# Attention, token mixer and gated feed-forward on one core: the first loads and the first chunks of attention in another order

## The chip, the cores and the metric

One core of a Trainium2 chip runs the whole program. The metric is the device time of one execution in microseconds (us); three runs of the kernel before took 794.02 to 795.17 us, with a median of 794.14 us.

## The reference

Inputs are q, k and v of shape (4, 8, 576, 64): 4 batches, 8 heads, 576 rows. Everything is float32 outside; the kernel works with pairs of float16 (a high and a low part) and with float32.

```python
scores = scale * q @ k^T                                # per batch and head, 576 x 576
scores = where(scores >= max(scores) - tau, scores, -1e9)
attn = exp(scores - max) ; attn /= sum(attn) + 1e-9
x = (attn @ v) with the heads side by side              # (4, 576, 512)
u = x + (relu(x^T @ w_tok1) @ w_tok2)^T                 # mixes the rows
x = u + relu(u @ w_ch1) @ w_ch2
h = relu(x @ w_in)
gate = sigmoid(conv3(h))                                # conv over rows, weights conv_w
out = (h * gate) @ w_out
```

## The kernel before

Attention runs over pairs of heads, four pairs for a batch, numbered 0 to 3 (a fifth pair is pair 0 of the next batch). A pair has nine chunks of 128 query rows, so a batch has 36 chunks, numbered 0 to 35 in batch 0. The generator `attention(b)` gives the steps of a chunk in a software pipeline, one chunk apart: `scores` (TensorE, L308), `exps` (the maximum on VectorE L324, the threshold and the exponential on ScalarE L334 and L336), `mask` (VectorE, L343), `ph` (the float16 high part on ScalarE, L348), `rest` (the low part on GpSimd, L352, then a DMA transpose issued from SyncE, L357), and five chunks later `pv` (TensorE, L367 and L370). The transposed chunk is what `pv` multiplies with v. After a pair's nine chunks, `norm` and `tok` (the token mixer, L407 and L422) follow. `dense(b)` is the rest of a batch on TensorE (L547, L565, L598, L621). For batch 0 attention runs alone; then `dense(b)` and `attention(b + 1)` are interleaved.

`prep(b, p)` brings a pair in: q (L236) and k (L240) by DMA, a scaling of q on ScalarE (L244), v by DMA (L268), then for each of the two heads a scaling of v on GpSimd (L272), its high part on ScalarE (L273) and its low part on GpSimd (L274). It stops (`yield`) between these, and `attention` runs the next piece in a later iteration.

`wload` brings a piece of the weights in: a DMA of 512 columns of 8 bytes (L118, three buffers `st`), a conversion on ScalarE and VectorE (L155 to L159), then a scaling on GpSimd (L143 or L153), the high part on ScalarE (L144) and the low part on GpSimd (L145). `W0` lists the steps of `attention(0)` at which a piece is begun.

A scheduler takes this program and sets the order on each engine; it pulls work ahead when its inputs and buffers are free. `tc.issue_after(x)` keeps what is written under it behind the instruction x. `hold` uses it to keep loads behind a transpose (`turn[i]` is the transpose of chunk i). On the chip each engine, and SyncE's queue of DMAs, works through its own order; an instruction that waits holds up all that stand behind it on its engine.

All DMAs of the first 100 us are issued by SyncE, shown as SPq.

Of the kernel before, what the change touches and what calls it, by code (L numbers as in the profile page):

```python
# [8 lines left out]
F32 = mybir.dt.float32  # L9
# [10 lines left out]
def kernel(ctx: ExitStack, tc: tile.TileContext, q, k, v, tau,  # L20
# [7 lines left out]
    nc = tc.nc  # L28
# [37 lines left out]
    V, A, G, T = nc.vector, nc.scalar, nc.gpsimd, nc.tensor  # L66


    one = const.tile([P, 1], F32, name="one")
    V.memset(one, 0.0)  # L70
    A.activation(out=one, in_=one, func=AF.Exp)
    idf = const.tile([P, P], F32, name="idf")
    make_identity(nc, idf)
    ident = const.tile([P, P], F16, name="ident")
    V.tensor_scalar_mul(ident, idf, 1.0 / UDS)
    ident2 = const.tile([P, 64], F16, name="ident2")
    V.tensor_tensor(out=ident2, in0=ident[:, 0:64], in1=ident[:, 64:P], op=ALU.add)
    blk = const.tile([P, 2, 1], F32, name="blk")
    V.memset(blk, 0.0)
    V.memset(blk[0:64, 0:1], 1.0)  # L80
    V.memset(blk[64:P, 1:2], 1.0)
    tau_t = const.tile([P, 1], F32, name="tau_t")
    nc.sync.dma_start(tau_t, tau.to_broadcast([P, 1]))

# [16 lines left out]
    wi = wpair([P, NG, NC, P], "wi")  # L103
    wo = wpair([P, NG, C], "wo")

    turn, behind, crit = {}, {}, {}

    def hold(x):
        return tc.issue_after(turn[behind[x]].ins) if behind.get(x) in turn else nullcontext()

    ps = psum.tile([P, 8, 512], F32, name="ps")
    CB = 4

    def load_hl(src, o, n):

        st = stage.tile([P, 512, 2], I32, tag="st", name="st")
        with hold("w"):
            nc.sync.dma_start(st[:, :n].rearrange("p n w -> p (n w)"), src.bitcast(I32)[:, 2 * o:2 * (o + n)])  # L118
        halves = st[:, :n].rearrange("p n w -> p (n w)").bitcast(U16).rearrange("p (n w) -> p n w", w=4)
        return halves[:, :, 1], st[:, :n, 1]  # L120
# [54 lines left out]
    def wnext():  # L175
        x = wq.pop(0)
        wrun.append(wload(*x, bank=6 if total - len(wq) <= W1 else CB))
        next(wrun[-1])

    def wstep(n):  # L180

        for _ in range(n):
            while wq and len(wrun) < 3:
                wnext()
            if wrun:
                next(wrun.pop(0))
            if wq:
                wnext()
        if n and not wrun and CB not in free:
            free.append(CB)  # L190

    cw = const.tile([P, 3 * NG], F32, name="cw")
    if conv_w.dtype == F32:
        nc.sync.dma_start(cw, conv_w)
    else:
        float32(cw, cw, *load_hl(conv_w, 0, 3 * NG), 0)
    cw = cw.rearrange("p (k g) -> p k g", k=3)


# [29 lines left out]
    def prep(b, p):  # L229

        vh, vl = v_t[p % 2]
        qt, kt = qk_t[p % 2]
        pair[b, p] = dict(qt=qt, kt=kt, vh=vh, vl=vl)
        if b < NB32:
            with hold("qk") if b else nullcontext():
                nc.sync.dma_start(f32(qt), q[b, p])  # L236
                for h in range(2):
                    if b == 0 and p < 2:
                        G.memset(f32(kt[h])[(1 - h) * D:(2 - h) * D], 0.0)
                    nc.sync.dma_start(f32(kt[h])[h * D:(h + 1) * D], k[b, p, h * D:(h + 1) * D])  # L240
            if b:
                yield
                yield
            A.activation(out=f32(qt), in_=f32(qt), func=AF.Copy, scale=qsc[:, 0:1])  # L244
        else:
            qn, kn = [qk2.tile([P, S], F32, tag="x", name="ld", bufs=15) for _ in range(2)]
            with hold("qk"):
                nc.sync.dma_start(qn, q[b, p])
                nc.sync.dma_start(kn, k[b, p])
        if b >= NB32:  # L250
            yield
            qs = qk2.tile([P, 2, S], F16, tag="x", name="qs", bufs=15)
            split(qs, qn, qsc[:, 1:2])
            for h in range(2):
                for x in range(2):
                    nc.sync.dma_start(qt[x * D:(x + 1) * D, h], qs[h * D:(h + 1) * D, x])
            yield
            ks = qk2.tile([P, 2, S], F16, tag="x", name="ks", bufs=15)
            split(ks, kn, QK)
            for h in range(2):  # L260
                for r in range(2):
                    nc.sync.dma_start(kt[h][r * D:(r + 1) * D], ks[h * D:(h + 1) * D])
        yield
        vn = []
        for hh in range(2):
            t = qk2.tile([P, S], F32, tag="x", name="ld", bufs=15)
            with hold("qk") if b else nullcontext():
                nc.sync.dma_start(t, v[b, 2 * p + hh])  # L268
            vn.append(t.rearrange("p (a d) -> p a d", d=D))
        yield  # L270
        for hh in range(2):
            G.tensor_scalar(out=vn[hh], in0=vn[hh], scalar1=VSC, scalar2=1.0, op0=ALU.mult, op1=ALU.mult)  # L272
            A.activation(out=vh[:, hh, :, 0:D], in_=vn[hh], func=AF.Copy)  # L273
            G.tensor_tensor(out=vl[:, hh], in0=vn[hh][:, 0:NS + 1], in1=vh[:, hh, 0:NS + 1, 0:D], op=ALU.subtract)  # L274
            yield
# [69 lines left out]
    def ph(i):  # L345
        c = chk[i]
        c["ph"] = half(i, 1) if i < PER else qk2.tile([P, 2 * S], F16, tag="x", name="ph", bufs=15)
        A.activation(out=c["ph"][:, 0:S], in_=c["e"], func=AF.Copy)  # L348

    def rest(i):  # L350
        c = chk[i]
        G.tensor_tensor(out=c["ph"][:, S:], in0=c["e"], in1=c["ph"][:, 0:S], op=ALU.subtract)  # L352
        if i < PER:
            c["pt"] = half(i, 2).rearrange("p (a b) -> p a b", b=P)
        else:
            c["pt"] = qk2.tile([P, NSL, P], F16, tag="x", name="pt", bufs=15)
        turn[i] = nc.sync.dma_start_transpose(out=c["pt"], in_=c["ph"])  # L357
# [40 lines left out]
    def tok(b, p):  # L398
# [36 lines left out]
        del pair[b, p]  # L435
        yield

    def steps(gen, names):

        while True:  # L440
            with ExitStack() as held:
                for x in names:
                    if x in crit:
                        held.enter_context(tc.issue_after(crit[x].ins))
                try:
                    next(gen)
                except StopIteration:
                    return
            yield

    def attention(b):
# [9 lines left out]
        for i in range(c0, c1, NSL):  # L461
            bb, p, _ = where(i + NSL)
            if bb < B:
                start(i - 1, prep(bb, p), (1, 2, 2, 1, 1, 1))
            start(i + NSL - 1 + lag + 2, tok(b, where(i)[1]), (2, 1, 1))
        if b == 0:
            for _ in prep(0, 0):
                pass
        i = c0 - 1
        while i < c1 + lag or todo:  # L470
            if c0 <= i < c1:
# [15 lines left out]
                    done.add(j)  # L487
            yield
            for g in todo.pop(i, ()):
                next(g, None)  # L490
            yield
            i += 1

# [155 lines left out]

    W0 = [0, 4, 8, 12, 16, 20, 24, 130]
    HW, HQ = 32, 35
    behind["qk"] = HQ
    for n, _ in enumerate(attention(0)):
        if n == 13:
            behind["w"] = HW
        wstep(W0.count(n))
    na, nq = n + 1, 2 * NF + 6 * NC + 2 * NG + 4 * (NS + 1)
    for b in range(B):  # L660
        att = attention(b + 1) if b + 1 < B else iter(())
# [66 lines left out]
```

## Time and profile before

| what | value |
|---|---|
| median of three runs | 794.14 us |
| profiled execution, first to last instruction (its span) | 783.1 us |
| median less span | 11.0 us |
| TensorE busy | 731.0 us, 93% |
| VectorE, ScalarE, GpSimd busy | 493.8, 471.3, 423.0 us |
| first `rest` (chunk 0) to last `rest` of batch 0 (chunk 35) | 14.04 to 94.46 us |
| first matmul of `dense(0)` (L547) | 114.3 us |

The profile gives no time of its own for the profiled execution besides its span. What lies around the span is thus taken as the 11.0 us by which the median is longer, and a change of the span is counted one for one on the median.

The window view shows what each engine did in a stretch: busy time and, in brackets, the number of instructions, then the clock that TensorE was granted (1.00 is 2.4 GHz, 0.50 is 1.2 GHz), the busy share of the DMA engines and the GB/s that they moved. The DMA share is a sum over packets, several of which can be under way in one engine, so it can pass 1.

### The profile page before, as it was taken

To read this page: it belongs to the slowest core of one execution; us is meant where nothing else is said; L and a number is where in the kernel's file an instruction comes from. 1 tells how busy PE (TensorE), PEld (TensorE's weight loads), DVE (VectorE), ACT (ScalarE), POOL (GpSimd) and SP (SyncE) were. 2 spreads that over 40 slices of the span, in tenths; PEclk is the share of its full clock that TensorE was granted. 3 is DMA by queue.
4 is the path that set the end of the run, shared out by engine and by line. 5 is a ranking of instruction groups with operands and counts; after the bars stand their busy time and mean duration, and the time that the engine had idled before them with its cause. 6 is when DMAs were issued, how large, how long until landed. Compare 5 with 4: busy or idle time off the path is not lost. (4 is left out here: it accounts for less than half of the span.)

```text
span 783.1 us, 18470 instructions
## 1 busy us (share of the span) xinstructions
PE 731.0 (93%) x7388; PEld 554.2 (71%) x7388; DVE 493.8 (63%) x837; ACT 471.3 (60%) x998; POOL 423.0 (54%) x471
## 2 busy tenths in 40 slices
PE   5679978999987899999999999999999999999998
PEld 3457756778766675788887856788888756878764
DVE  5578876877677861666877980676876850323370
ACT  7789967876667762666656852676656741311371
POOL 5988889887786651355664950366564830000040
PEclk9999999999999999999999999999999999999999
DMA  8999998997987421668667412667664401000001
GB/s 282 187 241 189 173 233 190 215 245 204 229 212 171 89 35 42 142 146 159 130 142 156 84 40 76 127 144 156 146 129 76 77 15 48 1 1 2 1 1 61
DMA packets 195046, 97.84 MB, mean 125 GB/s; under 512 B 174096, under 2 KB 176656, under 8 KB 194960
## 3 DMA queue, kind: packets, MB, share of 16 engines
q1 hardware_dynamic: 194640, 96.39, 55.3%
q8 instruction: 58, 0.95, 0.5%
q10 hardware_dynamic: 320, 0.26, 0.1%
q14 instruction: 28, 0.23, 0.1%
HBM read 42.36 MB, written 4.72 MB: 60 GB/s over the span
## 5 line engine op out<-in xcount | busy, mean ns | idle before, releaser
L352 POOL TENSOR_TENSOR ph<-e,ph 128x576 f16<-128x576 f32 x108 | 141.3, 1308 | 94.3 <-ACT ph L348 87.4
L565 PE MATMUL ps<-act_t,wc_h 128*128 128x256 f16 (+1 forms) x768 | 149.0, 286 | 0.0
L324 DVE TENSOR_REDUCE nm<-ps 128x1 f32<-128x576 f32 x144 | 107.9, 752 | 44.1 <-PE ps L312 27.0
L588 POOL TENSOR_TENSOR act_t<-ct,act_t 128x576 f16<-128x576 f32 x32 | 46.6, 1456 | 138.8 <-ACT act_t L587 135.9
L547 PE MATMUL ps<-u_h,wc_h 128*128 128x256 f16 (+1 forms) x384 | 109.7, 286 | 0.8 <-DVE act_t L522 0.8
L565 PE MATMUL ps<-act_t,wc_l 128*128 128x256 f16 (+1 forms) x384 | 109.8, 286 | 0.0
L547 PE MATMUL ps<-u_h,wc_l 128*128 128x256 f16 (+1 forms) x384 | 109.6, 286 | 0.0
L547 PE MATMUL ps<-u_l,wc_h 128*128 128x256 f16 (+1 forms) x384 | 109.2, 286 | 0.0
L308 PE MATMUL ps<-kt,qt 128*128 128x288 f32 (+1 forms) x320 | 87.8, 433 | 18.6 <-DVE act_t L343 9.0
L343 DVE SCALAR_TENSOR_TENSOR e<-ps,thr,e 128x576 f32<-128x576 f32 x108 | 87.8, 813 | 21.1 <-POOL thr L332 9.4
L547 PEld LDWEIGHTS <-wc_h 128*128 128x128 f16 x768 | 75.1, 98 | 19.9 <-issue 1.3
L565 PEld LDWEIGHTS <-wc_h 128*128 128x128 f16 x768 | 74.9, 98 | 19.0 <-issue 0.5
L367 PE MATMUL ps<-vh,pt 128*128 128x65 f16 (+1 forms) x1080 | 71.9, 195 | 8.5 <-DMA pt<-ph 5.8
L598 PE MATMUL ps<-u_h,wi_h 128*128 128x256 f16 (+1 forms) x256 | 73.0, 286 | 6.4 <-ACT h L574 3.3
L583 DVE SCALAR_TENSOR_TENSOR ct<-h,cw,ct 128x576 f32<-128x576 f32 x64 | 68.4, 1069 | 14.8 <-ACT ct L581 14.3
L621 PE MATMUL ps<-wo_h,act_t 128*128 128x512 f16 x256 | 76.3, 379 | 1.5 <-DVE u_l L430 0.9
L367 PEld LDWEIGHTS <-pt 128*128 128x128 f16 (+1 forms) x1080 | 62.4, 101 | 18.3 <-DMA pt<-ph 10.2
L308 PEld LDWEIGHTS ps<-kt,qt 128*128 128x128 f32 (+1 forms) x320 | 50.5, 185 | 33.8 <-DVE act_t L343 12.7
L348 ACT ACTIVATE ph<-e 128x576 f16<-128x576 f32 x108 | 73.0, 676 | 2.1 <-DVE e L343 2.1
L598 PE MATMUL ps<-u_h,wi_l 128*128 128x256 f16 (+1 forms) x256 | 73.1, 286 | 0.0
L598 PE MATMUL ps<-u_l,wi_h 128*128 128x256 f16 (+1 forms) x256 | 73.1, 286 | 0.0
L621 PEld LDWEIGHTS <-act_t 128*128 128x128 f16 x384 | 36.7, 98 | 43.6 <-issue 1.7
(113 smaller groups left out, 1613.0 us busy)
## 6 DMA issues: line engine op xcount, KB each, us to landing
st<-in_moe_w_ch_dram SPq DMA_DIRECT2D x24, 512.0 KB, 4.3
ld<-in_v_dram SPq DMA_DIRECT2D x32, 288.0 KB, 3.6
kt<-ks SPq DMA_DIRECT2D x32, 144.0 KB, 2.7
st<-in_moe_w_in_dram SPq DMA_DIRECT2D x8, 512.0 KB, 4.7
st<-in_moe_w_out_dram SPq DMA_DIRECT2D x8, 512.0 KB, 4.5
out_dram<-ot SPq DMA_DIRECT2D x16, 256.0 KB, 2.0
qt<-in_q_dram SPq DMA_DIRECT2D x8, 288.0 KB, 3.6
kt<-in_k_dram SPq DMA_DIRECT2D x16, 144.0 KB, 3.7
```

The costliest lines, as they stand in the source:

```text
L308: T.matmul(s3[o:o + m, a], f32(st["qt"])[:, q0:q0 + m], f32(st["kt"][hh])[:, a * hn:(a + 1) * hn], start=True, stop=True)
L324: crit["max"] = V.tensor_reduce(out=nm, in_=c["s3"], axis=AX.XY, op=ALU.max, negate=True)
L343: crit["mask"] = V.scalar_tensor_tensor(out=e3, in0=c["s3"], scalar=c["thr"], in1=e3, op0=ALU.is_ge, op1=ALU.mult)
L348: A.activation(out=c["ph"][:, 0:S], in_=c["e"], func=AF.Copy)
L352: G.tensor_tensor(out=c["ph"][:, S:], in0=c["e"], in1=c["ph"][:, 0:S], op=ALU.subtract)
L367: T.matmul(dst[o:o + m], pt[:, j, o:o + m], vh[:, hh, j, 0:D + 1], start=(j == 0), stop=(j == NSL - 1))
L547: T.matmul(t, wc1[wx][:, f, c], u[c][ux][:, sl], start=(c == 0 and i == 0), stop=(c == NC - 1 and i == 2))
L565: T.matmul(t, wc2[wx][:, c, f], r_t(f, rx)[:, sl], start=(by_dve(c) and f == 0 and i == 0), stop=(f == NF - 1 and i == 2))
L583: V.scalar_tensor_tensor(out=ct, in0=ht[:, kk:kk + S], scalar=cw[:, kk, f:f + 1], in1=ct, op0=ALU.mult, op1=ALU.add)
L588: G.tensor_tensor(out=g_t(f, 1), in0=ct, in1=g_t(f, 0), op=ALU.subtract)
L598: T.matmul(t, wi[wx][:, f, c], u[c][ux][:, s0:s0 + n], start=(c == 0 and i == 0), stop=(c == NC - 1 and i == 2))
L621: T.matmul(t, g_t(f, gx)[:, j * P:(j + 1) * P], wo[wx][:, f], **lim)
```

## The change

- `tau` is loaded through ScalarE's queue, and `conv_w` at step 60 of `attention(0)`, so q of pair 0 is the first DMA on SyncE's queue. ScalarE's table load for the exponential stands behind its DMA.
- TensorE multiplies a block of zeros ten times (128 x 128 by 128 x 512, float16) into a bank that is written anew later. The zeros stand in a part of `wo`, which VectorE clears first.
- `prep(0, 0)` is not run through before the first chunk: its q and k, the v loads and the first three loads of weights (`wfill`) come first, and the copies of v become steps of chunks 0 and 1.
- In the first three iterations the pieces of `prep` and of the weights stand behind an instruction of the chunks (`later`): behind the exponential, the high part, the mask or the low part.
- The weight pieces start at step 10 instead of 0, four steps apart as before.
- The loads of pairs 2 and 3 of batch 0 stand behind the newest transpose (`last_turn`), and pair 1's start of v is moved by one iteration.

```diff
-    nc.sync.dma_start(tau_t, tau.to_broadcast([P, 1]))
+    A.dma_start(tau_t, tau.to_broadcast([P, 1]))
+    A.activation(out=one, in_=one, func=AF.Exp)
...
+    zeros = wo[0][:, 0]
+    V.memset(zeros, 0.0)
...
+    def last_turn(p):
+        return tc.issue_after(turn[max(turn)].ins) if p > 1 and turn else nullcontext()
...
+    for _ in range(10):
+        T.matmul(ps[:, 7], zeros[:, 0:P], zeros, start=True, stop=True)
...
+    def wfill():
+        while wq and len(wrun) < 3:
+            wnext()
...
-            with hold("qk") if b else nullcontext():
+            with hold("qk") if b else last_turn(p):
                 nc.sync.dma_start(f32(qt), q[b, p])
...
-            if b:
-                yield
+            for _ in range(2 if b else p > 0):
                 yield
...
-            with hold("qk") if b else nullcontext():
+            with hold("qk") if b else last_turn(p):
                 nc.sync.dma_start(t, v[b, 2 * p + hh])
...
+    def later(*names):
+
+        held = ExitStack()
+        for x in names:
+            held.enter_context(tc.issue_after(crit[x].ins))
+        return held
...
-                start(i - 1, prep(bb, p), (1, 2, 2, 1, 1, 1))
+                start(i - 1, prep(bb, p), (3 if i == 0 else 1, 2, 2, 1, 1, 1))
...
-            for _ in prep(0, 0):
-                pass
+            first = prep(0, 0)
+            next(first)
+            next(first)
+            wfill()
+            start(c0, first, (1, 1))
...
-                next(g, None)
+                with later("exp" if i == 0 else "ph") if 0 <= i < 3 else nullcontext():
+                    next(g, None)
...
-    W0 = [0, 4, 8, 12, 16, 20, 24, 130]
+    W0 = [10, 14, 18, 22, 26, 30, 34, 130]
...
-        if n == 13:
+        if n == 23:
             behind["w"] = HW
-        wstep(W0.count(n))
+        if n == 60:
+            conv_load(cw_all)
+        if n in W0:
+            with later("ph", "mask", "lo") if n < 20 else nullcontext():
+                wstep(1)
```

In the rows of the order below, line numbers are those of each kernel: L352, L272, L274, L143, L145 and L357 of before are L366, L286, L288, L151, L153 and L371 of the change.

The first place is GpSimd's queue, from the low parts of pair 0's v to the low part (`rest`) of chunk 2. `ld` is a loaded v, `vl` its low part, `act_t` a chunk, `wf` and `wt` a piece of the weights. Before:

```order
L274 TENSOR_TENSOR vl_154<-ld,vh_153 128x320 x2
L352 TENSOR_TENSOR act_t<-act_t 128x576
L272 TENSOR_SCALAR ld<-ld 128x576 x2
L143 TENSOR_SCALAR wf<-wf 128x512
L352 TENSOR_TENSOR act_t<-act_t 128x576
L272 TENSOR_SCALAR ld<-ld 128x576 x3
L274 TENSOR_TENSOR vl_156<-ld,vh_155 128x320
L272 TENSOR_SCALAR ld<-ld 128x576
L143 TENSOR_SCALAR wf<-wf 128x512
L274 TENSOR_TENSOR vl_156<-ld,vh_155 128x320
L272 TENSOR_SCALAR ld<-ld 128x576
L352 TENSOR_TENSOR act_t<-act_t 128x576
```

The same stretch in the change:

```order
L288 TENSOR_TENSOR vl_159<-ld,vh_158 128x320
L286 TENSOR_SCALAR ld<-ld 128x576
L366 TENSOR_TENSOR act_t<-act_t 128x576
L286 TENSOR_SCALAR ld<-ld 128x576
L288 TENSOR_TENSOR vl_159<-ld,vh_158 128x320
L366 TENSOR_TENSOR act_t<-act_t 128x576
L151 TENSOR_SCALAR wf<-wf 128x512
L288 TENSOR_TENSOR vl_161<-ld,vh_160 128x320 x2
L366 TENSOR_TENSOR act_t<-act_t 128x576
```

Five scalings of v and one scaling of weights have left the place between chunk 1's and chunk 2's low parts, and one scaling of pair 1's v now stands ahead of chunk 0's low part instead of behind it.

The second place is SyncE's queue from its start to the first transposes. Before:

```order
L83 DMA tau_t<-in_tau_dram 128x1
L118 DMA st<-in_moe_conv_w_dram 128x48
L236 DMA qt_157<-in_q_dram 128x576
...
L236 DMA qt_160<-in_q_dram 128x576
L240 DMA kt_0_161<-in_k_dram 64x576
L240 DMA kt_1_162<-in_k_dram 64x576
L268 DMA ld<-in_v_dram 128x576 x8
L357 DMA_TRANSPOSE act_t<-act_t 128x9x128
```

The same stretch in the change:

```order
L251 DMA qt_162<-in_q_dram 128x576
...
L251 DMA qt_165<-in_q_dram 128x576
L255 DMA kt_0_166<-in_k_dram 64x576
L255 DMA kt_1_167<-in_k_dram 64x576
L282 DMA ld<-in_v_dram 128x576 x2
L371 DMA_TRANSPOSE act_t<-act_t 128x9x128
```

Two DMAs ahead of q are gone, and six of the eight v loads ahead of the first transpose (those of pairs 2 and 3 and of the next batch's pair 0) are gone from there.

The third place is GpSimd's queue in the change, behind chunk 13's low part, where pair 2's v is now scaled and split:

```order
L286 TENSOR_SCALAR ld<-ld 128x576
L153 TENSOR_TENSOR wt_l<-wf,wt_h 128x288
L366 TENSOR_TENSOR act_t<-act_t 128x576
L161 TENSOR_SCALAR st<-st 128x512
L410 TENSOR_TENSOR xl<-x_324,xh 128x4x64
L286 TENSOR_SCALAR ld<-ld 128x576
L288 TENSOR_TENSOR vl_159<-ld,vh_158 128x320
```

Both scalings stood ahead of chunk 2's or chunk 3's low part before. On SyncE's queue in the change these two loads stand behind 11 transposes, those of pair 3 behind 20, and those of the next batch's pair 0 behind 27.

## Rows read from the trace of the kernel before

**Rows 1.** The page, its first line.

```profile
span 783.1 us, 18470 instructions
```

**Rows 2.** Window view, stretches of 10 us; columns as told above, GB/s last.

```profile
10.00:20.00 10.00, 6.38 (x26) 3.77 (x25) 9.42 (x14) 10.00 (x21) 6.11 (x8) 1.00 1.07 340
20.00:30.00 10.00, 5.20 (x40) 3.48 (x40) 5.33 (x9) 7.37 (x17) 9.27 (x12) 0.88 0.74 195
...
50.00:60.00 10.00, 8.81 (x118) 7.38 (x119) 7.19 (x15) 8.16 (x19) 8.57 (x10) 1.00 1.18 238
...
70.00:80.00 10.00, 10.00 (x147) 8.04 (x145) 8.06 (x16) 8.96 (x20) 7.87 (x8) 1.00 1.01 188
80.00:90.00 10.00, 9.54 (x147) 7.57 (x144) 9.38 (x18) 10.00 (x25) 8.81 (x11) 1.00 1.04 159
```

**Rows 3.** Timeline of SyncE's queue: start, duration, instruction.

```profile
0.72 0.39 SPq L83 DMA_DIRECT2D tau_t<-in_tau_dram  x1
...
1.63 0.43 SPq L236 DMA_DIRECT2D qt<-in_q_dram  x1
...
7.72 7.12 SPq L268 DMA_DIRECT2D ld<-in_v_dram  x8
```

**Rows 4.** Timeline of TensorE, the first scores and two later ones.

```profile
6.09 5.36 PE L308 MATMUL ps<-kt,qt 128*128 128x288 f32 x12 [6.09 <-ACT qt L244]
11.84 1.24 PE L308 MATMUL ps<-kt,qt 128*128 128x288 f32 x4 [0.40 <-DVE act_t L343]
...
28.08 2.29 PE L308 MATMUL ps<-kt,qt 128*128 128x288 f32 x4 [3.22 <-DVE act_t L343]
```

**Rows 5.** Timeline of GpSimd, chunk 0's to chunk 2's low part.

```profile
14.04 1.28 POOL L352 TENSOR_TENSOR act_t<-act_t 128x576 f16<-128x576 f32 x1 [3.40 <-ACT act_t L348]
...
17.60 1.28 POOL L352 TENSOR_TENSOR act_t<-act_t 128x576 f16<-128x576 f32 x1
18.97 2.17 POOL L272 TENSOR_SCALAR ld<-ld 128x576 f32<-128x576 f32 x3
21.22 0.77 POOL L274 TENSOR_TENSOR vl<-ld,vh 128x320 f16<-128x320 f32 x1
...
22.83 0.62 POOL L143 TENSOR_SCALAR wf<-wf 128x512 f32<-128x512 f32 x1
...
25.12 1.27 POOL L352 TENSOR_TENSOR act_t<-act_t 128x576 f16<-128x576 f32 x1
```

**Rows 6.** Waits of GpSimd from 20 to 60 us, longest first.

```profile
POOL act_t L352 <- ACT act_t L348: 2.5, 4, 0.9
```

**Rows 7.** DMA views: median landing of v (0:30) and q (30:60); v's spread.

```profile
ld<-in_v_dram SPq DMA_DIRECT2D x10, 288.0 KB, 6.0
...
qt<-in_q_dram SPq DMA_DIRECT2D x1, 288.0 KB, 3.3
...
DMA to landing us min/median/max: 4.2/6.0/7.4
```

**Rows 8.** Timelines of SyncE's queue and of GpSimd, three places from 45 to 83 us.

```profile
45.62 3.97 SPq L357 DMA_TRANSPOSE act_t<-act_t  x2
50.01 1.28 POOL L352 TENSOR_TENSOR act_t<-act_t 128x576 f16<-128x576 f32 x1
...
64.51 4.48 SPq L357 DMA_TRANSPOSE act_t<-act_t  x3
68.95 2.52 POOL L352 TENSOR_TENSOR act_t<-act_t 128x576 f16<-128x576 f32 x2
...
74.76 18.11 SPq L357 DMA_TRANSPOSE act_t<-act_t  x10
78.76 2.67 POOL L352 TENSOR_TENSOR act_t<-act_t 128x576 f16<-128x576 f32 x2 [0.36 <-ACT act_t L348]
81.39 1.06 POOL L396 TENSOR_TENSOR xl<-x,xh 128x256 f16<-128x256 f32 x2
```

**Rows 9.** Timeline of GpSimd between batch 0's last chunk and `dense(0)`.

```profile
103.74 0.67 POOL L153 TENSOR_SCALAR st<-st 128x512 f32<-128x512 f32 x1 [2.63 <-DMA st<-in_moe_w_ch_dram]
```

More of the change, by code (lines that the diff above doesn't have):

```diff
@@ L66 @@
     V, A, G, T = nc.vector, nc.scalar, nc.gpsimd, nc.tensor
-    one = const.tile([P, 1], F32, name="one")
-    V.memset(one, 0.0)
-    A.activation(out=one, in_=one, func=AF.Exp)
     idf = const.tile([P, P], F32, name="idf")
@@ L77 @@
     V.tensor_tensor(out=ident2, in0=ident[:, 0:64], in1=ident[:, 64:P], op=ALU.add)
+    one = const.tile([P, 1], F32, name="one")
+    V.memset(one, 0.0)
     blk = const.tile([P, 2, 1], F32, name="blk")
@@ L178, in wnext @@
         next(wrun[-1])
+    def wfill():
+        while wq and len(wrun) < 3:
+            wnext()
     def wstep(n):
         for _ in range(n):
-            while wq and len(wrun) < 3:
-                wnext()
+            wfill()
             if wrun:
@@ L192, with conv_load @@
     cw = const.tile([P, 3 * NG], F32, name="cw")
[L193 to L196, printed above, removed]
+    def conv_load(cw):
+        if conv_w.dtype == F32:
+            nc.sync.dma_start(cw, conv_w)
+        else:
+            float32(cw, cw, *load_hl(conv_w, 0, 3 * NG), 0)
+    cw_all = cw
     cw = cw.rearrange("p (k g) -> p k g", k=3)
@@ L347, in ph @@
         c["ph"] = half(i, 1) if i < PER else qk2.tile([P, 2 * S], F16, tag="x", name="ph", bufs=15)
-        A.activation(out=c["ph"][:, 0:S], in_=c["e"], func=AF.Copy)
+        crit["ph"] = A.activation(out=c["ph"][:, 0:S], in_=c["e"], func=AF.Copy)
     def rest(i):
         c = chk[i]
-        G.tensor_tensor(out=c["ph"][:, S:], in0=c["e"], in1=c["ph"][:, 0:S], op=ALU.subtract)
+        crit["lo"] = G.tensor_tensor(out=c["ph"][:, S:], in0=c["e"], in1=c["ph"][:, 0:S], op=ALU.subtract)
         if i < PER:
@@ L463, in attention @@
             if bb < B:
-                start(i - 1, prep(bb, p), (1, 2, 2, 1, 1, 1))
+                start(i - 1, prep(bb, p), (3 if i == 0 else 1, 2, 2, 1, 1, 1))
             start(i + NSL - 1 + lag + 2, tok(b, where(i)[1]), (2, 1, 1))
         if b == 0:
-            for _ in prep(0, 0):
-                pass
+            first = prep(0, 0)
+            next(first)
+            next(first)
+            wfill()
+            start(c0, first, (1, 1))
         i = c0 - 1
```

## The prediction

> **What bounds the kernel now.** I read the page first: its span is 783.1 us [rows 1], and 11.0 us lie around it up to the median of 794.14 us. The change touches only the first tenth of the program, so the next view is that of the windows there, and then the timelines of SyncE's queue, GpSimd and TensorE at the places where the order changes.
>
> In the windows [rows 2] the reader should look at who is full, and where that changes. From 20 to 30 us GpSimd is busy for 9.27 of 10 us while TensorE has 5.20 and ScalarE 7.37. From 50 to 60 us GpSimd still has 8.57. From 70 to 90 us TensorE is full (10.00 and 9.54), and GpSimd has 7.87 and 8.81. So attention of batch 0 has two parts: a first one, up to about chunk 18, at GpSimd's pace, and a second one at TensorE's. GpSimd's waits say the same: between 20 and 60 us it waited for the chunks' high parts for 2.5 us in all [rows 6].
>
> What GpSimd does in the first part is seen in its timeline [rows 5]. Chunk 0's low part starts at 14.04 us, chunk 1's at 17.60, and chunk 2's not before 25.12 us. In those 7.5 us it scales v for pairs that are needed 16 and more chunks later. The loads for these are eight in a row on SyncE's queue from 7.72 us on, for 7.12 us [rows 3]. Each low part is followed by a transpose, and without transposes TensorE has nothing to multiply with v: it waits 3.22 us ahead of 28.08 us, and then its four instructions of a chunk's scores take 2.29 us, where four took 1.24 us at 11.84 [rows 4]. The granted clock of 20 to 30 us is 0.88 as a mean of the two levels [rows 2].
>
> **The start.** tau (0.72) and conv_w are ahead of q, which is issued at 1.63 us [rows 3]; q will be issued at 0.72, 0.91 us earlier. The first twelve score instructions take 5.36 us, 0.45 us each, against 1.24 / 4 = 0.31 us later [rows 4], so they ran at the lower clock in part. The zeros occupy TensorE until about the time at which q is there (ten multiplications of 512 columns, at most 0.45 x 512 / 288 = 0.80 us each by the first scores' row, 8 us in all; at the least 0.31 x 512 / 288 / 4 = 0.14 us each, 1.4 us, since float16 needs fewer passes than float32). At the upper end the scores would start 3 us later, at the lower 0.9 us earlier.
>
> I take all of that as worth nothing, because something later ends last. In the new order of GpSimd one scaling of pair 1's v stands ahead of chunk 0's low part. That v load is the first of the eight, issued at 7.72 us, and v loads of this stretch landed in 6.0 us as a median and 7.4 at most [rows 3, 7]. It is queued right behind the weights, so I take 7.4: it landed at 15.1, and will at 14.2 after 0.91 us less. With a scaling of 2.17 / 3 = 0.7 us chunk 0's low part then starts at 14.9 us instead of 14.04, and chunk 1's at 14.9 + 1.28 + 0.7 + 0.77 = 17.6 us, which is where it is now [rows 5]. With 6.0 us the two would come 1.4 us earlier. Bounds of this term: a gain of 1.4 and a loss of 1.0 (zeros and scaling both late); value 0. What hides the start's gain is thus the landing of pair 1's v.
>
> **The main term.** Between the low parts of chunks 1 and 2 the new order has one weight scaling and two low parts of v: 17.6 + 1.28 + 0.62 + 2 x 0.77 = 21.0 us instead of 25.12, so 4.1 us earlier [rows 5]. I check it by counting all of GpSimd's work ahead of chunk 2's low part: five scalings of v (0.67 to 0.72 each) and one of weights (0.62) fewer, 4.0 us. Up to chunk 18's low part, where GpSimd's part ends, the new order has six scalings of v instead of ten and six low parts instead of seven, and as many weight pieces: 4 x 0.67 + 0.77 = 3.45 us less work. This is the term that I use: a gain of 3.45 us at chunk 18.
>
> GpSimd's waits of 2.5 us [rows 6] lie in part where TensorE had slept and come back at the lower clock (2.29 against 1.24 us, 1.0 us). With transposes coming earlier, this should go in part: bounds 0 and 2.5, value 1.0.
>
> **What comes back.** The four scalings and the low part, 3.45 us, and two more scalings for the next batch are now done behind chunk 18. There TensorE sets the pace, and GpSimd has 2.13 and 1.19 us free in the two stretches of 70 to 90 us alone [rows 2]. I cost this at nothing; if TensorE did not cover it, all 3.45 us would be given back. SyncE issues six v loads between transposes now, for about 0.4 us each [rows 3], nothing while it waits for low parts. The weights move by two or three chunks and stay in number; conv_w's small conversion moves behind chunk 33; nothing.
>
> From chunk 18 on everything moves by the gain, as the pace there is TensorE's. Ahead of dense(0) the last low part of pair 3's attention output stands behind two scalings of weights that wait for a load, instead of one. One costs 0.67 us, and waited for 2.63 us for its load [rows 9]; bounds 0.67 and 3.3, value 0.65. dense(0) and what follows start by the difference earlier, and since nothing in them is changed but for the scheduler's order, I pass it on whole.
>
> Sum: 0 + 3.45 + 1.0 + 0 - 0.65 = 3.8 us. The time is 794.14 - 3.8 = 790.3 us.
>
> **A rule that speaks against it.** The Trainium skill (DMA: Bandwidth & Descriptors, Rules for kernel authors) says to issue a DMA early, compute meanwhile, and wait for it late. The loads of pairs 2 and 3 are issued later here; by that rule the order of before is the better one, and the first rival below would be the outcome. In this trace the early loads brought early scalings with them, so the trace agrees with the rule only as to the loads.
>
> **Rivals.** *Late v loads hold up GpSimd (slower).* A scaling of v now stands between low parts, and GpSimd can't pass it. I compare the time between the issue of such a load and the scaling, with the pace of before [rows 8]. Pair 2: transpose 10 is the first of two from 45.62, issued by 46.9 at about 1.3 us; GpSimd is through chunk 13 at 51.3: 4.4 us. Pair 3: transpose 19 is the first of three from 64.51 and is out at 66.0; GpSimd is there at 71.5: 5.5 us. Next batch: transpose 26 is the third of ten, out at 80.2; GpSimd is there at 81.4 and 1.06 us of folds later, at 82.5: 2.3 us. With a landing of L us the stalls sum to 3L - 12.2 once L passes 5.5. At q's 3.3 us for the same 288 KB between transposes there is 1.0 us, which the free time covers [rows 2, 7]. At the 6.0 of the early v loads it is 5.8, and the time 790.3 + 5.8 = 796.1 us; at 7.4 it is 10.0, and 800.3 us. It is slower by over 0.2% from L = 5.9 on. For it: the DMA share is 1.01 to 1.18 in all these stretches. Against it: q's landing in the middle of them.
>
> *The DMA engines are the bound (no change).* They have a share of 1 or more from 50 to 60 and 70 to 90 us. Six v loads, 6 x 0.295 = 1.77 MB, move from a stretch in which they hid behind the start into one that is full. At the 340 GB/s of 10 to 20 us [rows 2] that is 5.2 us, so the gain of 3.8 turns into a loss of 1.4, or into about nothing if half of it is covered: 793 to 795.5 us. For it: the share; against it: 188 and 159 GB/s while transposes ran, and a share that passes 1 without a ceiling to be seen.
>
> *The gain grows (faster).* If chunk 0 gains its 1.4 us, TensorE stays at 2.4 GHz, and all of GpSimd's waits go, the sum is 1.4 + 3.45 + 2.5 - 0.65 = 6.7 us: 787.4 us. For it: ScalarE ended chunk 2's high part well ahead of its low part, as GpSimd did not wait there [rows 5]. Against it: other waits take the place of those removed, on ScalarE, which was full from 80 to 90 us.
>
> **How the numbers follow.** The forecast, with 2 to 5.5 us gained, has a chance of 0.50; the larger gain 0.17; no change 0.21, the DMA's case; slower 0.12, the late loads'. 0.2% is 1.6 us, about what a measurement of this kernel can tell from no change. Faster by that is the first two: 0.67; same 0.21; slower 0.12. The range reaches from a little beyond the larger gain, 786.2, over the case of no change to 795.2 us; about 1 in 10 lies above it, and 1 in 10 below. The likeliest case's own range is 788.6 to 792.1 us.
>
> **What would show it.** Right: chunk 1's low part near 17.6 us, chunk 2's near 21, chunk 18's some 4 us earlier, dense(0) near 110.5 instead of 114.3 us; GpSimd idle for less than 1 us ahead of any scaling of v behind chunk 13. Wrong: chunk 0's low part long behind 15 us; GpSimd waiting for `ld`; chunk 18 early but chunk 35 as late as now (94.5 us), which is the DMA's case; or dense(0) early and its end late, by the scheduler's order in between.

## The result, and the profile after

The change is slower: 797.84 us, the median of five runs (797.34 to 798.95), beside 794.14 us for the kernel before on the same chip (five runs, 791.54 to 795.17). The ratio is 1.0065, with a 95% interval from 1.0041 to 1.0090. The forecast was 790.3 us, and its range ended at 795.2.

One number of the working falls at once. The profiled execution of the change took 798.35 us, and its span is:

```profile
span 796.5 us, 18513 instructions
```

So 1.85 us lie around the span, not 11.0. A later run of the kernel before took 788.68 us with a span of 786.9, again 1.8 us. The span of 783.1 us [rows 1] thus belonged to an execution of about 785 us, an uncommonly quick one: 82 runs of the kernel before, taken beside the experiments below, lie at 786.03 to 795.08 us. The later run (e1 below) is used as a second profile of before. Both are quicker than the median of their kernel, so the spans in the table differ by more (9.6 and 13.4 us) than the medians (3.7 us).

The start of the low part (`rest`) of some chunks, the first matmul of the two dense parts and the span, in us, read from the timelines of each kernel:

| kernel | 0 | 1 | 2 | 8 | 14 | 18 | 24 | 29 | 35 | 36 | dense(0) | dense(1) | span |
|---|---|---|---|---|---|---|---|---|---|---|---|---|---|
| before, first profile | 14.0 | 17.6 | 25.1 | 37.6 | 52.6 | 60.6 | 72.8 | 82.4 | 94.5 | 98.1 | 114.3 | 316.4 | 783.1 |
| before, second (e1) | 14.0 | 17.6 | 25.1 | 37.7 | 52.8 | 61.0 | 73.1 | 82.8 | 94.8 | 98.4 | 116.8 | 320.1 | 786.9 |
| the change | 16.6 | 19.5 | 23.0 | 35.5 | 51.1 | 62.1 | 77.7 | 91.2 | 102.8 | 106.3 | 121.0 | 329.7 | 796.5 |

The gain was there: chunks 2, 8 and 14 came 1.5 to 2.2 us earlier. By chunk 18 it had turned into a loss of 1.1 to 1.5, and by chunk 36 into one of 7.9 to 8.2 us. From there to dense(1) another 1.7 us went against the second profile (5.1 against the first). That part says little: in five profiles with the order of before (the two here, e12, e16 and e17 below) this stretch took 218.3 to 224.3 us, and in the change 223.4, while chunk 36 came at 98.1 to 99.3 us in the five and at 106.3 in the change. From dense(1) to the end all three take 466.7 or 466.8 us. So the loss to be explained is the one ahead of chunk 36.

GpSimd's timeline of the change at the start:

```profile
15.88 0.67 POOL L286 TENSOR_SCALAR ld<-ld 128x576 f32<-128x576 f32 x1 [5.62 <-DMA ld<-in_v_dram]
16.63 1.27 POOL L366 TENSOR_TENSOR act_t<-act_t 128x576 f16<-128x576 f32 x1
...
19.47 1.28 POOL L366 TENSOR_TENSOR act_t<-act_t 128x576 f16<-128x576 f32 x1
20.83 0.62 POOL L151 TENSOR_SCALAR wf<-wf 128x512 f32<-128x512 f32 x1
21.53 1.49 POOL L288 TENSOR_TENSOR vl<-ld,vh 128x320 f16<-128x320 f32 x2
22.98 1.27 POOL L366 TENSOR_TENSOR act_t<-act_t 128x576 f16<-128x576 f32 x1
```

It answers to [rows 5]. From chunk 1 to chunk 2 it takes 3.51 us now (7.52 before): the scalings are gone from there as forecast. But chunk 0 stands behind a scaling that waited 5.62 us for pair 1's v.

Where the gain is given back is seen in SyncE's timeline of the change:

```profile
0.73 0.40 SPq L251 DMA_DIRECT2D qt<-in_q_dram  x1
...
7.27 1.74 SPq L282 DMA_DIRECT2D ld<-in_v_dram  x2
...
61.95 1.45 SPq L251 DMA_DIRECT2D qt<-in_q_dram  x1
63.44 1.13 SPq L255 DMA_DIRECT2D kt<-in_k_dram  x2
64.75 5.06 SPq L371 DMA_TRANSPOSE act_t<-act_t  x3
69.86 1.09 SPq L282 DMA_DIRECT2D ld<-in_v_dram  x2
71.07 9.22 SPq L371 DMA_TRANSPOSE act_t<-act_t  x5
80.34 0.78 SPq L251 DMA_DIRECT2D qt<-in_q_dram  x1
81.18 1.14 SPq L255 DMA_DIRECT2D kt<-in_k_dram  x2
82.43 3.12 SPq L371 DMA_TRANSPOSE act_t<-act_t  x2
85.60 2.01 SPq L282 DMA_DIRECT2D ld<-in_v_dram  x2
```

and in three timelines further on, of GpSimd (66 to 69 and 90 to 92 us) and of ScalarE (77 us):

```profile
66.77 1.28 POOL L366 TENSOR_TENSOR act_t<-act_t 128x576 f16<-128x576 f32 x1
...
76.88 0.68 ACT L362 ACTIVATE act_t<-act_t 128x576 f16<-128x576 f32 x1 [2.03 <-DMA act_t<-act_t]
...
77.70 1.28 POOL L366 TENSOR_TENSOR act_t<-act_t 128x576 f16<-128x576 f32 x1 [1.46 <-ACT act_t L362]
...
90.42 0.67 POOL L286 TENSOR_SCALAR ld<-ld 128x576 f32<-128x576 f32 x1 [2.63 <-DMA ld<-in_v_dram]
91.17 1.28 POOL L366 TENSOR_TENSOR act_t<-act_t 128x576 f16<-128x576 f32 x1
```

Chunk 20's low part ends at 68.05. But the queue had issued loads of q and k from 61.95 to 64.57, is still at the three transposes behind them, and then issues two loads of v for 1.09 us: chunk 20's transpose goes out at 71.07, 3 us after its low part. ScalarE's next high part at 76.88 then waits 2.03 us for a transpose, GpSimd waits for that, and chunk 24 is 4.9 us later than in the first profile of before (chunk 23 was 2.5 us later). At 90.42 it is GpSimd itself that waits 2.63 us for the v that was issued at 85.60.

From chunk 18 to chunk 35 the change takes 40.7 us, and both profiles of before take 33.8. The waits of ScalarE for transposes and of GpSimd for v in that stretch of the change (window 62 to 103 us; in total, times, longest) are:

```profile
ACT act_t L362 <- DMA act_t<-act_t: 4.2, 6, 2.0
...
POOL ld L286 <- DMA ld<-in_v_dram: 2.6, 1, 2.6
```

Neither row is there in the two profiles of before. Together they are 6.8 us, beside the 6.9 us that the stretch is longer; waits of two engines need not add up, so this is a sign and no proof. Waits of TensorE and GpSimd from 0 to 95 us in the change (in total, times, longest); the row of TensorE was 7.4, 10, 1.6 in the first profile of before, and that of GpSimd 3.9, 1, 3.9:

```profile
PE ps L381 <- DMA act_t<-act_t: 14.5, 9, 5.2
...
POOL ld L286 <- DMA ld<-in_v_dram: 12.6, 4, 5.6
```

The windows of the change that answer to [rows 2], with TensorE at 6.68 us between 50 and 60 (8.81 before), and 7.68 and 7.22 between 70 and 90 (10.00 and 9.54 before): TensorE no longer sets the pace there. From 56.1 to 59.5 us it was also granted 1.2 GHz.

```profile
10.00:20.00 10.00, 3.77 (x16) 1.79 (x14) 6.72 (x10) 8.35 (x18) 4.13 (x6) 0.76 0.61 159
20.00:30.00 10.00, 7.03 (x56) 5.01 (x57) 4.90 (x7) 7.43 (x16) 9.29 (x10) 0.73 0.74 152
50.00:60.00 10.00, 6.68 (x63) 4.98 (x63) 4.69 (x7) 5.40 (x13) 8.92 (x12) 0.83 1.14 226
70.00:80.00 10.00, 7.68 (x96) 5.68 (x95) 6.43 (x12) 7.23 (x15) 8.04 (x9) 1.00 1.09 202
80.00:90.00 10.00, 7.22 (x118) 5.47 (x116) 6.46 (x13) 7.91 (x19) 6.43 (x7) 1.00 1.08 192
```

### The profile page after: what moved, and what is told of

It is laid out like the page before. It is cut to its first block, busy times and chain, and to the rows that moved or that the text cites. A ratio compares the mean times of both kernels' runs of the same rounds, so it can differ in the third digit from the quotient of the medians.

```text
span 796.5 us, 18513 instructions
## 1 busy us (share of the span) xinstructions
PE 742.0 (93%) x7398; PEld 557.5 (70%) x7398; DVE 494.1 (62%) x838; ACT 471.1 (59%) x998; POOL 421.8 (53%) x471
## 5 line engine op out<-in xcount | busy, mean ns | idle before, releaser
L366 POOL TENSOR_TENSOR ph<-e,ph 128x576 f16<-128x576 f32 x108 | 141.7, 1312 | 96.0 <-ACT ph L362 90.1
L322 PE MATMUL ps<-kt,qt 128*128 128x288 f32 (+1 forms) x320 | 91.7, 441 | 12.9 <-DVE act_t L357 8.0
L357 DVE SCALAR_TENSOR_TENSOR e<-ps,thr,e 128x576 f32<-128x576 f32 x108 | 87.7, 812 | 20.7 <-POOL thr L346 9.9
L623 PE MATMUL ps<-u_h,wi_h 128*128 128x256 f16 (+1 forms) x256 | 73.1, 286 | 5.2 <-DVE u_l L444 3.0
L381 PEld LDWEIGHTS <-pt 128*128 128x128 f16 (+1 forms) x1080 | 62.3, 101 | 16.2 <-DMA pt<-ph 9.1
L623 PE MATMUL ps<-u_h,wi_l 128*128 128x256 f16 (+1 forms) x256 | 73.1, 286 | 0.0
L322 PEld LDWEIGHTS ps<-kt,qt 128*128 128x128 f32 (+1 forms) x320 | 51.1, 188 | 31.1 <-DVE act_t L357 13.0
```

The lines of the kernel that those rows point to most:

```text
L322: T.matmul(s3[o:o + m, a], f32(st["qt"])[:, q0:q0 + m], f32(st["kt"][hh])[:, a * hn:(a + 1) * hn], start=True, stop=True)
L357: crit["mask"] = V.scalar_tensor_tensor(out=e3, in0=c["s3"], scalar=c["thr"], in1=e3, op0=ALU.is_ge, op1=ALU.mult)
L366: crit["lo"] = G.tensor_tensor(out=c["ph"][:, S:], in0=c["e"], in1=c["ph"][:, 0:S], op=ALU.subtract)
L381: T.matmul(dst[o:o + m], pt[:, j, o:o + m], vh[:, hh, j, 0:D + 1], start=(j == 0), stop=(j == NSL - 1))
L623: T.matmul(t, wi[wx][:, f, c], u[c][ux][:, s0:s0 + n], start=(c == 0 and i == 0), stop=(c == NC - 1 and i == 2))
```

## The experiments

Ratios are to the kernel before on the same chip, with their 95% interval. The letters of theories are told in each expectation. Some expectations count the rows that stand elsewhere in an engine's order than in before; of GpSimd's 477 the change moves 109, and e9 below 43.

### First set: the hold and the zeros

**e1_before_again** is the kernel before, profiled once more.

> The kernel before, unchanged, profiled once more beside the other runs of this set. If its first profile (span 783.1 us, one stretch at the lower TensorE clock in the middle of the program) is typical, the span comes out within 2 us of that, and the 11 us between span and median lie around the span. If that profile was an uncommonly quick execution, the span is near 792 us, with more stretches at the lower clock (mean granted clock below 0.995), and the change costs about 4 us rather than the 13 us between the two profiles.

788.68 us, span 786.9; its chunks are in the table above, within 0.4 us of the first profile. What differs is TensorE's clock. Apart from the last 2 us, in which it had no work left, it was granted 1.2 GHz in one stretch only in the first profile, 27.6 to 31.0 us; in the second also in these two (window view; the granted clock is the third number from the right):

```profile
109.50:112.90 3.40, 3.21 (x23) 2.93 (x23) 2.49 (x5) 1.31 (x5) 3.24 (x5) 0.50 0.77 146
246.10:249.50 3.40, 3.40 (x16) 1.42 (x14) 2.37 (x8) 1.43 (x3) 1.88 (x3) 0.50 1.23 326
```

That is 6.8 us at half the clock, and the stretch from chunk 36 to dense(1) was 3.4 us longer (221.7 against 218.3) with the same waits. So one order gives executions that lie some us apart. The span lies between the two that the expectation names.

**e2_no_hold** is the change without `last_turn`:

```diff
-        return tc.issue_after(turn[max(turn)].ins) if p > 1 and turn else nullcontext()
+        return nullcontext()
```

> The change without the hold: the loads of pairs 2 and 3 no longer wait for a transpose; all else as in the change. Theory A (the late loads and the scalings that come late with them hold up GpSimd from chunk 14 on, which lost 6 us between chunk 10 and chunk 24 and 4 more at chunk 29): ratio 0.990 to 0.995 to before, 4 to 8 us below the change, chunk 35's low part before 95 us. Theory B (the start, where GpSimd waited 12.6 us for v of pairs 0 and 1, costs the time): still 1.003 to 1.007. Theory C (what is lost is lost at the lower TensorE clock, wherever it falls): the time follows the number of stretches at the lower clock, whatever the order.

802.90 us, 1.0133 [1.0101, 1.0165]. Chunk 2 at 26.6, 18 at 66.8, 36 at 110.1 us. Without the hold the change is some 5 us slower still, against theory A: the hold isn't the whole cost, and the parts beside it cost more alone.

**e3_no_zeros** is the change without the ten multiplications and the clearing of their block.

> The change without the ten multiplications of zeros and without the clearing of their operand. Theory A: no change against the change itself, 1.004 to 1.009 to before. Theory C (the zeros bring TensorE to the higher clock early, and it falls back for 10.2 us at 15 us, when the chunks stall): 1.000 to 1.004, with the first scores 2 us longer and the stretch at the lower clock shorter. Theory B: as A.

797.42 us, 1.0071 [1.0047, 1.0096]. Chunk 0 came at 12.3 us and chunk 36 at 100.2, 6.1 us earlier than in the change, but dense(1) at 329.0, as late as in the change. What the first chunks gained did not arrive.

**e4_hold_alone** is the kernel before with `last_turn` on the loads of pairs 2 and 3:

```diff
-            with hold("qk") if b else nullcontext():
+            with hold("qk") if b else last_turn(p):
                 nc.sync.dma_start(f32(qt), q[b, p])
...
-            with hold("qk") if b else nullcontext():
+            with hold("qk") if b else last_turn(p):
                 nc.sync.dma_start(t, v[b, 2 * p + hh])
```

> The kernel before with the hold alone: loads of pairs 2 and 3 behind the newest transpose; start, zeros and weights as before. Theory A: slower, 1.004 to 1.010, chunk 2's low part earlier than 25.1 us, chunk 24's and 35's later than in the kernel before. Theory B: 0.993 to 0.999, since chunk 1's and 2's low parts are no longer behind the scalings of v. Theory C: follows the clock.

794.79 us, 1.0053 [1.0028, 1.0078]. Chunk 2 at 21.8 and chunk 8 at 34.2 us, 3.3 and 3.5 us earlier than in e1: this is the main term of the prediction, alone, and near the size forecast. It is given back between chunks 8 and 11 (10.5 us, 7.2 in e1), 20 and 23 (8.1 us, 5.8 in e1), and 32 and 35 (11.8 us, 6.5 in e1), where held loads or the scalings behind them stand; chunk 36 is at 104.8. That is what theory A had forecast.

### Second set: late loads, late scalings, late weights

My theory (A) was now that late loads of v hold up transposes and GpSimd; the rivals that late work on GpSimd costs by itself (B), or that the start and the weights do (C).

**e5_scale_late** loads all of v early, and keeps only the scalings behind the low parts:

```diff
-            G.tensor_scalar(out=vn[hh], in0=vn[hh], scalar1=VSC, scalar2=1.0, op0=ALU.mult, op1=ALU.mult)
+            with tc.issue_after(crit["lo"].ins) if b == 0 and p > 1 else nullcontext():
+                G.tensor_scalar(out=vn[hh], in0=vn[hh], scalar1=VSC, scalar2=1.0, op0=ALU.mult, op1=ALU.mult)
```

> The kernel before, with all loads of v early as in before; only the scalings of v of pairs 2 and 3 stand behind the newest low part (the order has them behind the low parts of chunks 11, 13, 20 and 22 instead of 2). This takes apart what the hold of the loads does in one. Theory A (late loads: a v load between transposes delays transposes and lets GpSimd wait): the early gain of the hold, 3 to 4 us at chunks 2 to 8, comes and stays; no jump of over 1 us at chunks 13 and 22; chunk 35 near 91, dense(0) near 113, 786 to 789 us where before has 791. Theory B (late work on GpSimd: a scaling costs where it stands, since GpSimd has no time to spare behind chunk 12 either): the gain is given back in jumps of 1.5 to 3 us at chunks 11 to 14 and 20 to 23; chunk 35 at 95 or later, and 791 to 795 us.

796.44 us, 1.0086 [1.0064, 1.0108]. Chunk 2 at 22.3, 8 at 38.1, 14 at 54.2, 18 at 64.2, 35 at 98.1 us. The gain of 2.8 us is gone by chunk 8, ahead of the first late scaling (42.67 us), and 2.8 us more go up to chunk 18; from 18 to 35 it takes 33.9 us, as e1 does (33.8), though pair 3's scalings stand there: late scalings alone cost nothing in that stretch. Neither theory fits: the time is above both ranges, and part of the loss lies where nothing of this edit stands yet. In GpSimd's and TensorE's timelines of e5 ahead of chunk 8 the reader sees a wait for a transpose:

```profile
38.13 2.51 POOL L353 TENSOR_TENSOR act_t<-act_t 128x576 f16<-128x576 f32 x2 [3.34 <-ACT act_t L349]
...
36.66 0.22 PE L368 MATMUL ps<-vh,act_t 128*64 128x65 f16 x1 [3.27 <-DMA act_t<-act_t]
```

**e6_change_v_early** is the change with the same edit, and v of pairs 2 and 3 not held.

> The change, but v of pairs 2 and 3 loads early and its scalings stand behind the newest low part; q and k of these pairs stay held behind transposes. Theory A (late v loads are what costs): the jumps at 14 to 15, 23 to 24 and 28 to 29 fall from 9 us in sum to under 4, chunk 35 near 97, 791 to 793 us. Theory B (late scalings on GpSimd): the jumps stay near the scalings, chunk 35 near 102, 796 to 799 us. Theory C (neither; the start and the weights' move cost, as without the hold, where chunk 18 came 6 us late): chunk 18 behind 62 and 797 to 801 us.

799.09 us, 1.0114 [1.0083, 1.0144]. In the first 95 us the waits fall, as theory A has it (e6's rows of those shown for the change):

```profile
PE ps L382 <- DMA act_t<-act_t: 8.7, 9, 3.0
...
POOL ld L287 <- DMA ld<-in_v_dram: 7.9, 3, 4.3
```

Chunk 35 comes at 97.6 (forecast 97), and chunk 36 at 99.8, 6.5 us earlier than in the change. Of that, 2.9 us are left at dense(1), since the stretch up to there grew from 223.4 to 227.0 us. And the time is no better: the profiled execution, 795.02 us, is the quickest of six, and the others took 797.44 to 802.69. Where those lost more is not shown. So the late loads of v explain a large part of the change's jumps, but taking them away moved the order again and did not shorten the time.

**e7_weights_later** is the kernel before with the weights' steps of the change:

```diff
-    W0 = [0, 4, 8, 12, 16, 20, 24, 130]
+    W0 = [10, 14, 18, 22, 26, 30, 34, 130]
...
-        if n == 13:
+        if n == 23:
```

> The kernel before with the list of the weights' steps alone as in the change (ten steps later). Theory C (the weights' later place is the cost that is left without the hold): chunk 18 at 63 or later where before has 60.6, and 795 us or more. Otherwise, chunk 18 within 1 us of before and within 2 us of before's time, 789 to 793 us.

802.74 us, 1.0158 [1.0128, 1.0188]; chunk 18 at 62.4, 29 at 86.6, 35 at 102.6 us. Theory C's time came true, its place (chunk 18 at 63 or later) not quite. From chunk 29 to chunk 32 it takes 12.3 us (5.5 in e1), and one wait stands there, for a weight instead of a v, but of the same kind. SyncE's and GpSimd's timelines:

```profile
82.84 9.56 SPq L357 DMA_TRANSPOSE act_t<-act_t  x5
92.50 0.55 SPq L118 DMA_DIRECT2D st<-in_moe_w_ch_dram  x1
...
98.28 0.64 POOL L153 TENSOR_SCALAR st<-st 128x512 f32<-128x512 f32 x1 [3.50 <-DMA st<-in_moe_w_ch_dram]
98.88 2.51 POOL L352 TENSOR_TENSOR act_t<-act_t 128x576 f16<-128x576 f32 x2
```

The load stands behind five transposes on its queue, its scaling ahead of low parts on GpSimd.

**e8_change_weights_first** is the change with the list of before (0, 4, 8 ...).

> The change with the list of the weights' steps as in before (0, 4, 8 ...), all else as in the change. Theory C: the loss goes down by 3 us or more, to 793 to 795 us. Theories A and B: the jumps behind chunk 14 stay, 796 to 799 us.

800.03 us, 1.0120 [1.0097, 1.0142]. Theory C falls as a sum of parts: the weights' move costs 12 us alone, and taking it out of the change gains nothing.

### Third set: the parts of the start, and a nearly empty edit

The hold alone and the weights alone cost 0.53 and 1.58%, together three times the whole change. The third set asks whether an edit costs by what it does (T1), or because it moves the order (T2). **e9_conv_late_alone** moves the load of conv_w (24 KB in the profile, not 6) and its conversion to step 60, and nothing else:

```diff
+        if n == 60:
+            conv_load(cw_all)
```

> The kernel before with conv_w's load (6 KB, one small conversion) at step 60 and nothing else; the scheduler's order moves a little behind it (on TensorE 535 of 14299 rows, on GpSimd 43 of 477). Theory T1 (the change loses where GpSimd waits for a load that was issued behind transposes): nothing of that is here, so 789 to 792 us where before has about 790.5, and a ratio within 0.2%. Theory T2 (the order of before is a good one by itself, and whatever moves it costs, by more time at TensorE's lower clock and longer waits in batch 0's attention and dense(0)): 794 to 798 us.

797.10 us, 1.0069 [1.0040, 1.0097]. Chunk 36 is at 99.3 us (98.4 in e1): the loss is behind it, where from there to dense(1) it takes 227.8 us instead of 221.7. TensorE's waits there, before's first profile (98 to 316 us) and then e9 (99 to 327), show transposes and masks coming later:

```profile
PE ps L367 <- DMA pt<-ph: 5.8, 8, 1.7
PE ps L308 <- DVE e L343: 3.3, 4, 2.3
```

```profile
PE ps L370 <- DMA pt<-ph: 11.3, 9, 3.6
PE ps L311 <- DVE e L346: 7.9, 6, 3.6
```

In the four other profiles with the order of before the two are 5.7 to 7.3 and 3.1 to 4.3 us.

**e10_zeros_alone** is the kernel before with the zeros, **e11_start_alone** the change without the hold and with the old weights' list.

> The kernel before with the ten multiplications of zeros and the clearing of their block alone. The loads of v stay early; the order moves on TensorE in 1665 rows. T1: 789 to 792 us, chunk 0's low part 14 to 16 us. T2: 794 to 798 us, with the loss spread over chunks 3 to 36 and dense(0).

800.37 us, 1.0114 [1.0084, 1.0144]; chunk 0 at 18.4, chunk 36 at 103.8 us. Two scalings of pair 1's v had moved ahead of chunk 0's low part, and waited 2.02 us for it.

> The change's start alone (tau and conv_w moved, zeros, pair 0's copies as steps, weights' conversions behind chunk 0's); no load of v held, the weights' steps as in before. T1: chunk 0 at 15 to 18 us (one scaling of pair 1's v ahead of it), given back by chunk 18, no GpSimd wait for a load behind chunk 3 of over 1 us, 789 to 793 us. T2: 795 to 800 us.

802.54 us, 1.0130 [1.0100, 1.0160]; chunk 0 at 18.1, chunk 36 at 109.7 us, with no load of v held. Both e10 and e11 lie above what either theory gave them.

**e12_tau_alone** issues tau from ScalarE's queue. Beside it only ScalarE's table load and the clearing of its operand move, at the start:

```diff
-    nc.sync.dma_start(tau_t, tau.to_broadcast([P, 1]))
+    A.dma_start(tau_t, tau.to_broadcast([P, 1]))
+    A.activation(out=one, in_=one, func=AF.Exp)
```

> The kernel before with tau's load through ScalarE's queue alone: every engine's order stays as it is, SyncE has one load less ahead of q (0.45 us). T1 and T2 both: within 0.2% of before, 789 to 792 us, chunk 0 between 13.4 and 14.2. If the time differed by over 3 us here as well, not the order but the instant at which work begins (against TensorE's clock) would set the time, and T2 would be wrong in its cause.

788.69 us, 0.9971 [0.9949, 0.9994], a little below what both theories gave it. The only part that leaves the order as it was, but for these, is the only one that isn't slower.

### Fourth set: three more orders

**e13_hold_qk_only** puts `last_turn` on q and k alone (the first hunk of e4). **e14_conv_at_step_20** is e9 with step 20. **e15_q_first** adds to e12 conv_w's load on ScalarE's queue, so that q is the first load on SyncE's.

> The kernel before, with q and k of pairs 2 and 3 held behind the newest transpose and v loaded early as in before. T1 (only loads that GpSimd waits for ahead of low parts cost): 789 to 792 us, chunk 36 within 1.5 us of before's 98.4. T2 (whatever moves the order costs): 794 to 799 us, with no single wait to blame.

794.99 us, 1.0068 [1.0040, 1.0095]; chunk 36 at 105.5 us.

> The kernel before with conv_w's load at step 20 instead of at the start: the same work, in an order that differs on TensorE in 1321 rows. T1: 789 to 792 us. T2: 794 to 800 us.

796.30 us, 1.0075 [1.0048, 1.0103]; chunk 36 at 104.9 us.

> The kernel before with tau's and conv_w's loads on ScalarE's queue, so that q is the first load on SyncE's, and the conversion of conv_w where it was: the order differs on TensorE in 1589 rows. T1: chunk 0 near 13.5 to 14 us, 787 to 791 us. T2: 794 to 799 us, wherever chunk 0 begins.

797.44 us, 1.0081 [1.0052, 1.0109]; chunk 0 at 13.8, chunk 36 at 104.7 us.

All three times are as theory T2 has them. e13 holds no v, and loses as much as e4, which does. But it is not without a wait to blame: from chunk 18 to chunk 35 ScalarE waits 4.8 us for transposes, as it does in the change (4.2) and in e4 (3.8), and not at all in the two profiles of before. Held loads of q and k are enough for that.

### Fifth set: the order kept

**e16_order_kept** clears one small tile twice; no other row moves. **e17_tau_alone_again** is e12 beside it.

> The kernel before with one more clearing of a small tile on VectorE at the start; no row of any engine's order moves. T2 (a moved order is what costs): within 0.2% of before, 789 to 792 us. If this too were 4 us slower, any edit at all would cost, and the order would not be the reason.

790.67 us, 1.0006 [0.9986, 1.0025].

> Tau's load on ScalarE's queue alone, beside e16 on the same chip. If the gain of 0.3% is real: a ratio of 0.995 to 0.999 to before, and 1.5 to 3 us below e16. If it was chance: within 0.2% of both.

789.20 us, 0.9979 [0.9955, 1.0002]. The gain is 2.3 us in e12 and 1.7 in e17, whose interval just reaches 1: small if real, and the profiles of e12 and e17 (chunk 36 at 99.3 and 98.3 us) don't show its place. It is the best version that was found, some 7 us below the change by the ratios.

## Why the prediction was wrong

**The step that failed** is "What comes back", costed at nothing, with the sentence "From chunk 18 on everything moves by the gain, as the pace there is TensorE's." Between chunks 18 and 35 the change lost 6.9 us (40.7 us against 33.8). The cover was TensorE's pace, and it went as soon as transposes came late: TensorE was busy 14.90 us of 70 to 90 us, where [rows 2] have 19.54. SyncE's issue of the held v loads was costed at "nothing while it waits for low parts", and at about 0.4 us for each load of v, which is q's row of [rows 3]; the row of v there is 7.12 us for eight, 0.89 each. In the change two loads of v take 1.09 us at one place and 2.01 at another, and a group of q and k 2.6. The issue time was weighed for the queue, and not for who waits behind it: finished low parts whose transposes stand behind the loads, and then ScalarE, which waited 4.2 us for transposes. GpSimd's wait for one held v is the other 2.6 us.

**The first rival**, late v loads, at a chance of 0.12, gave the sign, and 796.1 us at a landing of 6.0 us. Its mechanism, GpSimd waiting for loads that land late, is the smaller part of what happened. The six held loads landed in 3.7 us as a median (3.1 to 6.4), near q's 3.3 and not at 6.0; GpSimd waited for one of the six, 2.63 us. That the rival's time lies near 797.84 us is luck. e6 takes the late loads of v away: from 18 to 35 it needs 36.7 us, so 4.0 of the 6.9 us go, and ScalarE's wait for transposes falls from 4.2 to 0.9 us. The rule of the Trainium skill that was weighed there (DMA: Bandwidth & Descriptors, Rules for kernel authors: issue a DMA early) agrees with e6's trace up to chunk 36. It decided nothing about the time: e5 and e6 load v early and are slow as well.

**The main term** was right in mechanism where it was read: 3.51 us between chunks 1 and 2 (forecast 3.4), 2.1 us earlier at chunk 2 in the change, 3.3 to 3.5 alone (e4). It was wrong that the gain reaches chunk 18. From chunk 8 to chunk 18 the change took 26.6 us, e1 23.3: pair 2's scalings stand there, as was counted, but ScalarE also waited 2.65 us for a transpose at 54.95 us.

**The start**, costed at 0, lost 1.9 to 2.6 us, more than its bound of 1.0. The reason given was right (pair 1's v lands last), its landing was not: issued at 7.27 us, the scaling could start at 15.88, 8.6 us later, where 7.4 was taken as the most. q was issued 0.90 us earlier, but that v only 0.45. In e15 q is first without the scaling ahead of chunk 0, and chunk 0 gains 0.2 us. That the first scores "ran at the lower clock in part" no row shows: the window view has a granted clock of 1.00 from 0 to 10 us.

**The waits of 1.0 us** with TensorE's lower clock did not go. The change was at 1.2 GHz from 15.2 to 25.4 us instead of 27.6 to 31.0. In the order of before such a stretch cost little: e16 was at 1.2 GHz for 13.6 us between 16.2 and 36.7 and has chunk 36 at 99.3 us, within 0.9 of e1.

**dense(0)**: the tail, costed at -0.65, is hidden in the 8 us by which chunk 36 is late; dense(0) began 4.2 us later than in e1, though nearer to chunk 36 (14.7 us behind it against 18.4).

**The order as a price of its own.** What follows chunk 36 was passed on whole, "since nothing in them is changed but for the scheduler's order". In the change this held as well as the profiles can tell (223.4 us up to dense(1)). In others it did not: in e3, e6 and e9, for example, the stretch took 227.0 to 228.8 us, more than in any of the five profiles with the order of before. Thirteen kernels beside the change moved the order, eight made from before and five from the change, and all thirteen were slower, by 0.53% to 1.58%; the three runs of kernels that kept it gave 0.9971, 1.0006 and 0.9979. Moving one load of 24 KB (e9, e14) costs 0.69 and 0.75%, as much as the whole change, 0.65%. One thing goes with it in all the traces: up to chunk 36, ScalarE and TensorE together waited 9.0 to 12.1 us for transposes in the five profiles with the order kept, and 12.5 to 23.4 us in the fourteen with it moved (21.7 in the change). Shown is that this holds for the orders tried. Not shown is what makes the order of before so much better than its neighbours, or whether that is chance: e2, e10 and e11 hold no v and still take 37.9 to 39.1 us from chunk 18 to chunk 35, and no run made the time of an order better by mending one of its waits.

**The span's neighbourhood** of 11.0 us came from one quick execution and a median of others. It did not enter the difference that was forecast, but it hid that executions of one order differ by up to 9 us, more than the gain. Over the 82 runs of before, a mean granted clock lower by 0.010 goes with 3.8 us more (a straight line; correlation 0.58). The change's clock was 0.985 as a mean of five runs, before's 0.988 over the 82: about 1 us of its loss by that line, which says nothing of cause.

The **rival of the DMA engines' share** is not supported: in the windows shown of 50 to 60 and 70 to 90 us their share is 1.08 to 1.14 in the change and 1.01 to 1.18 before. It predicted chunk 18 early, and that was late.

## What to carry to other kernels

Where a scheduler sets the order, first time two edits that do next to nothing: one that leaves every engine's order as it is, and one that moves it with the same work. Here the first gave 1.0006 and the second 1.007, so a forecast of -0.5% worked out from the edit's own instructions was smaller than what a moved order cost by itself. And on a queue that works in order, cost a load by what stands behind it: loads put between transposes were paid for here by whoever needed the next transposes (4.2 us) more than by the engine that reads the load (2.6 us).

## What the runs showed of the hardware

TensorE's lower clock falls in different places in executions of one and the same order (27.6 us alone; then 27.6, 109.5 and 246.1 us), and what goes with it differs by place: 6.8 us of it between chunk 36 and dense(1) in e1 went with 3.4 us more, and 13.6 us of it in the first chunks of e16 with under 1 us. It doesn't set the time alone: e17, with 3.4 us of it between chunk 36 and dense(1), took 4.5 us more there than the first profile of before.

The multiplications of zeros took 0.42 us each (ten in 4.15 us, ended at 5.39), and the first twelve scores behind them 3.15 us instead of the 5.36 of [rows 4]. They took 3.15 us in e10 and e11 too, which have the zeros, and 5.10 in e3, which is the change without them. TensorE was faster for them, and nothing came of it, as pair 1's v decided when chunk 0 could go on:

```profile
1.24 4.15 PE L120 MATMUL ps<-wo_h 128*128 128x512 f16 x10 [1.24 <-DVE wo_h L107]
5.74 3.15 PE L322 MATMUL ps<-kt,qt 128*128 128x288 f32 x12 [0.36 <-ACT qt L258]
```
